# W1 in thirds on two queues, four first units around tile 1's transposes, and a new order of single-tile and paired units up to tile 5

**Chip, cores, metric.** One core of one Trainium2 chip. The time is the device time of that core in microseconds (us). The kernel was already tuned: 207.95 us (median of 3 runs, 207.95 to 208.64) before the change.

## The reference

```python
# x: (1, 2048, 640) bf16; H = 32 heads of 20; F = 1536
xn  = layernorm(x)                                  # no scale, no bias
qkv = xn @ wqkv;  phi(t) = where(t > 0, t + 1, exp(t)) + 1e-6
A   = (phi(q) (phi(k)^T v)) / (phi(q) sum(phi(k)))  @ wo      # linear attention, per head
B   = gelu(xn @ w1 + b1) @ w2 + b2                  # dense block
out = x + A + B
```

## The kernel before

A small planner records instructions for each engine in program order. Each has resources that it reads and writes; the planner makes semaphore waits of them. x comes in 16 tiles of 128 tokens. First, the loads and the start of the dense block: each tile is normalised on VectorE (DVE; the power for rstd, one over the standard deviation, on POOL), transposed on TensorE (PE) and copied to `xnT` (tiles 0 to 3; the others are transposed by DMA), and multiplied with W1. That product is called h below, and k counts the five slices of 128 columns of D that are summed for it. A *unit* is 5 matmuls (k = 0..4) for 128 columns of F and one or more tiles, with its Gelu on ScalarE (ACT).

```python
dma_x(0, 1)
dma_w("scalar", b1tmp[:], ..., r_b1tmp)
dma_w1(0, "scalar")            # W1 in four quarters of 480 KB
dma_x(1, 1); dma_w1(1); dma_x(2, 1); dma_w1(2); dma_x(3, 1); dma_w1(3)
...                            # x tiles 4 to 15

def h_first(jbs):              # tile 0, k 0,1 of all units first, then k 2..4
    bs = [take(1) for _ in jbs]
    for (ks, res) in (((0, 1), r_xnTA), ((2, 3, 4), r_xnT[0])):
        for jb, b in zip(jbs, bs):
            Pl.ins("tensor", [... matmul(bank(b, 0, P), W1[:, k, ...], xnT[:, k, 0:P]) for k in ks],
                   reads=[r_W1[jb * P // FW], res], writes=[B_[b]])
    ...                        # Gelu of each unit

filler(10)                     # warm-up matmuls, N = 512
ln_stats(0); ln_half(1, 0); ln_half(1, 1); ln_aggr(1)
norm0(0, CA, r_xnA); norm0(CA, D, r_xnB)      # tile 0 in two parts
...                            # transposes, copies: first part DVE, second ACT
b1_step(); ln_norm(1)
h_first([0, 1, 2])
```

Second, `units(t0, n, lo, hi)`: units lo..hi of n tiles from t0 on. The last tile's output goes out in three stores (80, 48 and 32 KB), and the program waits for all stores. ACT, which has no work since 133 us, has these waits, but for the last:

```python
stores = [ev for (waits, fns, ev, dma) in Pl.records["sync"][n_sync:] if dma]   # 18
for ev in stores[:-1]:
    Pl.wait_event("scalar", ev)
Pl.wait_event("sync", stores[-1])
```

## Time and profile before

| | before |
|---|---|
| span of the profiled run | 206.8 us, clock 1.0 |
| PE / DVE / ACT busy | 98% / 54% / 35% |
| wait of the chain before PE's first real matmul | W1's first quarter, landed 6.98 us |
| first matmul of the K projection (chain; its own start in the timeline is 60.26) | 60.42 us |
| last DVE instruction | 205.04 to 205.33 us |
| from there to the end of the span | 1.50 us |

The chain names PE for 96% of the span. From 7.03 to 205.02 us it is PE alone, so each us that PE loses there moves the end. The first fence is the view of DMA issues from 200 to 207 us (size, us from issue to landing), the second SyncE's waits of the last four us (us in total, times, longest).

```profile
out_dram<-out_sb SPq DMA_DIRECT2D x1, 48.0 KB, 1.5
out_dram<-out_sb SPq DMA_DIRECT2D x1, 32.0 KB, 1.4
```

```profile
SPq L108 <- DMA out_dram<-out_sb: 1.1, 1, 1.1
```

The last 32 KB take 1.4 us from issue to landing, and the kernel ends when SyncE has seen that.

### The profile page before, as it was taken

How to read it: one execution, taken by the hardware profiler on the slowest of the kernel's cores; microseconds unless marked ns; L12 is line 12 of the kernel's file. 1: busy time of each engine (PE TensorE's matmuls, PEld its weight loads, DVE VectorE, ACT ScalarE, POOL GpSimd, SP SyncE). 2: the span in 40 equal slices, each digit the busy share in tenths (PEclk: the TensorE clock that was granted, in tenths of full speed). 3: DMA queues.
4: the chain of work that ended last, by engine and by line, in shares of the span. 5: the costliest groups of instructions: out<-in, count | busy, mean ns of one | idle time of the engine just before them, and what ended most of it. 6: DMA issues, size and time to landing. Idle time of an engine off the chain costs nothing.

```text
span 206.8 us, 3936 instructions
## 1 busy us (share of the span) xinstructions
PE 203.7 (98%) x1588; PEld 140.6 (68%) x1588; DVE 112.2 (54%) x231; ACT 73.2 (35%) x141; POOL 21.2 (10%) x59
## 2 busy tenths in 40 slices
PE   7999999999999999999999999999999999999996
PEld 2799987444457777777756556677777777777775
DVE  4679970000006888999288888574763522522332
ACT  2589887666676555111153554400000000000000
POOL 3245568000022000000000000000000000000000
PEclk9999999999999999999999999999999999999999
DMA  6999668998000000000300001932112112000002
GB/s 167 344 357 114 105 126 138 375 325 277 3 0 0 0 0 3 0 3 0 63 0 5 0 0 23 370 120 51 63 67 57 55 43 57 32 33 35 32 33 65
DMA packets 23851, 18.32 MB, mean 89 GB/s; under 512 B 10392, under 2 KB 23832, under 8 KB 23832
## 3 DMA queue, kind: packets, MB, share of 16 engines
q1 hardware_dynamic: 23152, 17.57, 30.1%
q10 hardware_dynamic: 680, 0.49, 0.9%
q8 instruction: 12, 0.20, 0.4%
q14 instruction: 7, 0.06, 0.1%
HBM read 12.62 MB, written 2.62 MB: 74 GB/s over the span
## 4 chain that ended last, share of the span: by engine, by line
PE 96%; DMA 3%; ACTq 0%; DVE 0%; issue 0%
PE ps L615 34%; PE ps L352 25%; PE ps L512 11%; PE ps L473 11%; PE ps L524 10%; DMA W<-in_B_w_dram 3%; PE ps L651 2%; PE ps L551 1%; PE ps L533 1%; PE ps L562 1%; PE ps L382 1%; PE ps L336 0%; ACTq L233 0%; DVE out_sb L654 0%
## 5 line engine op out<-in xcount | busy, mean ns | idle before, releaser
L352 PE MATMUL ps<-xnT,W 128*128 128x128 bf16 (+2 forms) x435 | 52.0, 282 | 0.0
L615 PE MATMUL ps<-W,HG 128*128 128x320 bf16 x360 | 51.0, 299 | 0.0
L352 PEld LDWEIGHTS ps<-xnT,W 128*128 128x128 bf16 x435 | 35.6, 98 | 15.6
L615 PEld LDWEIGHTS ps<-W,HG 128*128 128x128 bf16 x360 | 35.1, 98 | 14.2 <-issue 0.4
L356 ACT ACTIVATE HG<-ps,b1c 128x128 bf16<-128x128 f32 (+2 forms) x87 | 40.1, 493 | 12.4 <-PE ps L352 10.3
L634 DVE TENSOR_TENSOR out_sb<-ps,xnT 128x640 bf16<-128x640 f32 x15 | 12.4, 825 | 35.0 <-PE ps L615 34.8
L460 ACT ACTIVATE ek<-ps 128x512 bf16<-128x512 f32 (+1 forms) x36 | 23.2, 645 | 20.3 <-PE ps L524 10.6
L461 DVE TENSOR_SCALAR ek<-ek 128x512 bf16<-128x512 bf16 (+1 forms) x36 | 11.0, 304 | 33.7 <-ACT ek L460 32.5
L615 PE MATMUL ps<-Msb,PQ 128*128 128x320 bf16 x150 | 22.3, 299 | 0.0
L524 PE MATMUL ps<-xnT,Wqkv 128*128 128x512 bf16 x100 | 21.9, 379 | 0.0
L512 PE MATMUL ps<-xPK,xn_tm 128*128 128x320 bf16 x160 | 21.9, 299 | 0.0
L473 PE MATMUL ps<-Wqkv,xnT 128*128 128x320 bf16 x160 | 21.9, 299 | 0.0
L473 PEld LDWEIGHTS ps<-Wqkv,xnT 128*128 128x128 bf16 x160 | 15.7, 98 | 6.2
L512 PEld LDWEIGHTS ps<-xPK,xn_tm 128*128 128x128 bf16 x160 | 15.7, 98 | 6.1
L615 PEld LDWEIGHTS ps<-Msb,PQ 128*128 128x128 bf16 x150 | 14.7, 98 | 5.7
L524 PEld LDWEIGHTS ps<-xnT,Wqkv 128*128 128x128 bf16 x100 | 11.7, 117 | 9.5
L463 DVE SCALAR_TENSOR_TENSOR PQ<-ps,ek 128x512 bf16<-128x512 f32 x20 | 13.8, 692 | 2.1
L308 DVE BATCH_NORM_STATS2 stats<-xPK 128x6 f32<-128x320 bf16 x32 | 13.6, 467 | 1.9 <-DMA xPK<-in_A_x_dram 1.9
L463 DVE SCALAR_TENSOR_TENSOR xPK<-ps,ek 128x640 bf16<-128x640 f32 x16 | 13.2, 824 | 1.7
L499 DVE TENSOR_TENSOR Msb<-Msb,xPK 128x640 f32<-128x640 f32 x14 | 11.6, 826 | 0.5
L318 POOL TENSOR_TENSOR rstd<-aggr,mhalf 128x1 f32<-128x1 f32 x16 | 9.1, 569 | 8.9 <-DVE aggr L316 8.9
L516 ACT ACTIVATE W<-ps 128x640 bf16<-128x640 f32 x5 | 3.5, 704 | 18.2 <-PE ps L512 18.2
(61 smaller groups left out, 94.6 us busy)
## 6 DMA issues: line engine op xcount, KB each, us to landing
xnT<-in_A_x_dram SPq DMA_DIRECT2D x4, 640.0 KB, 6.2
Wqkv<-in_A_wqkv_dram SPq DMA_DIRECT2D x3, 800.0 KB, 6.5
out_dram<-out_sb SPq DMA_DIRECT2D x15, 160.0 KB, 1.8
W<-in_B_w_dram SPq DMA_DIRECT2D x1, 1920.0 KB, 15.2
W<-in_B_w_dram SPq DMA_DIRECT2D x3, 480.0 KB, 6.7
xPK<-in_A_x_dram SPq DMA_DIRECT2D x2, 640.0 KB, 9.0
Wo<-in_A_wo_dram SPq DMA_DIRECT2D x1, 800.0 KB, 10.4
xPK<-in_A_x_dram SPq DMA_DIRECT2D x4, 160.0 KB, 4.1
```

The source lines that it names most:

```text
L308: Pl.ins(v, lambda e: e.bn_stats(stats[:, s, 6 * h:6 * h + 6], x_in[:, t, h * HW:(h + 1) * HW]), reads=[r_x[t]], writes=[r_stats[s][h]])
L352: Pl.ins("tensor", [(lambda e, k=k: e.matmul(bank(b, 0, w), W1[:, k, jb * P:(jb + 1) * P], xnT[:, k, tok], start=(k == 0), stop=(k == DT - ...
L356: Pl.ins("scalar", lambda e: e.activation(HG[:, jb, tok], bank(b, 0, w), ACT.Gelu_apprx_tanh, bias=b1c[:, jb:jb + 1]), reads=[B_[b], r_b1c ...
L460: Pl.ins("scalar", lambda e: e.activation(e2, src, ACT.Exp), reads=br, writes=[r_ek[s]])
L461: Pl.ins(v, lambda e: e.tensor_scalar(et, et, 1.0, 1e-6, ALU.min, ALU.add), reads=[r_ek[s]], writes=[r_ek[s]])
L463: Pl.ins(v, lambda e: e.scalar_tensor_tensor(out=d2, in0=src, scalar=0.0, in1=e2, op0=ALU.max, op1=ALU.add), reads=br + [r_ek[s]], writes= ...
L473: fns.append(lambda e, k=k, h=h, b=b, t=t: e.matmul(bank(b + h, 0, HW), xnT[:, k, t * P:(t + 1) * P], Wqkv[:, k, D + h * HW:D + (h + 1) * ...
L499: Pl.ins(v, lambda e, t=t: e.tensor_tensor(out=zsum, in0=zsum, in1=PK[:, t, :], op=ALU.add), reads=[r_PK[t], r_zsum], writes=[r_zsum])
L512: Pl.ins("tensor", [(lambda e, t=t, h=h, b=b, f=f: e.matmul(bank(b + h, 0, HW), xn_tm[:, t, f * P:(f + 1) * P], PK[:, t, h * HW:(h + 1) * ...
L524: Pl.ins("tensor", [(lambda e, k=k, j=j, b=b: e.matmul(bank(b), Wqkv[:, k, j:D:DT], xnT[:, k, cc], start=(k == 0), stop=(k == DT - 1))) fo ...
L615: return lambda e: e.matmul(bank(b + h, 0, HW), l, r[:, h * HW:(h + 1) * HW], start=(i == 0), stop=(i == JT + DT - 1))
L634: Pl.ins(v, lambda e: e.tensor_tensor(out=halves(out_sb[:, s, :]), in0=pair(b), in1=halves(x_res[:, t, :]), op=ALU.add), reads=B_[b:b + 2] ...
```

## The change

The intent: PE waits for 480 KB of W1 until 6.98. The change splits a first third (640 KB) over the two queues, so that the part with k 0,1 is there early. It gives PE four units of tile 0 with tile 1's transposes in between, brings tile 0's normalisation and the bias's transpose forward, swaps the engines of tile 0's two copies, moves the statistics of the next tile behind the normalisation, in part, from tile 2 on, and reorders the units up to tile 5.

```diff
@@ -202,7 +202,8 @@
         r_xb = [R_("xb%d" % t) for t in range(NT)]
         r_xn = [R_("xn%d" % t) for t in range(NT)]
         r_xnT = [R_("xnT%d" % t) for t in range(NT)]
-        NW1 = 4
+        NW1 = 3
+        r_W1A = R_("W1_0A")
         r_W1 = [R_("W1_%d" % i) for i in range(NW1)]
         r_Wq, r_Wk, r_Wv, r_W2, r_Wo = R_("Wq"), R_("Wk"), R_("Wv"), R_("W2"), R_("Wo")
         r_b1tmp, r_b1c, r_b2 = R_("b1tmp"), R_("b1c"), R_("b2")
@@ -237,15 +238,16 @@
         FW = F // NW1
         def dma_w1(i, eng="sync"):
             dma_w(eng, W1[:, :, i * FW:(i + 1) * FW], w1v[:, :, i * FW:(i + 1) * FW], r_W1[i])
+        KA = 2
         dma_x(0, 1)
         dma_w("scalar", b1tmp[:], B_b1.rearrange("(a p) -> a p", p=P), r_b1tmp)
-        dma_w1(0, "scalar")
+        dma_w("scalar", W1[:, 0:KA, 0:FW], w1v[:, 0:KA, 0:FW], r_W1A)
         dma_x(1, 1)
+        dma_w("sync", W1[:, KA:DT, 0:FW], w1v[:, KA:DT, 0:FW], r_W1[0])
         dma_w1(1)
         dma_x(2, 1)
         dma_w1(2)
         dma_x(3, 1)
-        dma_w1(3)
         dma_x(4, 2)
         dma_x(6, 2)
         for c in range(2, NC):
@@ -375,14 +377,16 @@
                    reads=[res, r_ident], writes=[B_[b]])
             return xnT[:, k0:k1, 0:P], pT[:, 0:(k1 - k0) * P].rearrange("p (k q) -> p k q", k=k1 - k0), b
 
-        def h_first(jbs):
+        def h_first(jbs, between):
             bs = [take(1) for _ in jbs]
             for (ks, res) in (((0, 1), r_xnTA), ((2, 3, 4), r_xnT[0])):
                 for jb, b in zip(jbs, bs):
                     Pl.ins("tensor", [(lambda e, k=k, jb=jb, b=b: e.matmul(
                         bank(b, 0, P), W1[:, k, jb * P:(jb + 1) * P], xnT[:, k, 0:P],
                         start=(k == 0), stop=(k == DT - 1))) for k in ks],
-                        reads=[r_W1[jb * P // FW], res], writes=[B_[b]])
+                        reads=[r_W1A if res is r_xnTA else r_W1[jb * P // FW], res], writes=[B_[b]])
+                    if res is not r_xnTA and jb == jbs[1]:
+                        between()
             for jb, b in zip(jbs, bs):
                 Pl.ins("scalar", lambda e, jb=jb, b=b: e.activation(
                     HG[:, jb, 0:P], bank(b, 0, P), ACT.Gelu_apprx_tanh, bias=b1c[:, jb:jb + 1]),
@@ -391,21 +395,22 @@
         r_xnTA = R_("xnT0A")
         Pl.ins("scalar", lambda e: e.activation(b1c[:, 0:1], warm[:, 0:1], ACT.Gelu_apprx_tanh),
                reads=[r_warm], writes=[r_b1c])
-        filler(10)
+        filler(6)
+        b1_step()
+        filler(3)
         ln_stats(0)
         ln_half(1, 0)
         ln_half(1, 1)
-        ln_aggr(1)
         norm0(0, CA, r_xnA)
         norm0(CA, D, r_xnB)
+        ln_aggr(1)
         dA, sA, bA = transp0(0, 2, r_xnA)
         filler(1)
         dB, sB, bB = transp0(2, DT, r_xnB)
-        Pl.ins(v, lambda e: e.tensor_copy(dA, sA), reads=[B_[bA]], writes=[r_xnTA])
-        Pl.ins("scalar", lambda e: e.activation(dB, sB, ACT.Copy), reads=[B_[bB]], writes=[r_xnT[0]])
-        b1_step()
+        Pl.ins("scalar", lambda e: e.activation(dA, sA, ACT.Copy), reads=[B_[bA]], writes=[r_xnTA])
+        Pl.ins(v, lambda e: e.tensor_copy(dB, sB), reads=[B_[bB]], writes=[r_xnT[0]])
         ln_norm(1)
-        h_first([0, 1, 2])
+        h_first([0, 1, 2, 3], lambda: xnT_copy(1, transp(1)))
 
         TD = 4
         late = Pl.records["sync"][x_done:]
@@ -419,25 +424,25 @@
         def ln_next(t):
             if t + 1 < NT:
                 ln_half(t + 1, 0)
-                ln_half(t + 1, 1)
             ln_norm(t)
             if t + 1 < NT:
+                ln_half(t + 1, 1)
                 ln_aggr(t + 1)
 
-        xnT_copy(1, transp(1))
+        units(1, 1, 0, JQ)
+        units(0, 2, JQ, 2 * JQ + 1)
         ln_stats(2)
-        ln_next(2)
-        units(0, 1, 3, 2 * JQ)
-        units(1, 1, 0, 2 * JQ)
-        units(0, 2, 2 * JQ, 2 * JQ + 2)
+        ln_norm(2)
+        ln_stats(3)
         xnT_copy(2, transp(2))
-        units(0, 2, 2 * JQ + 2, JT)
+        units(0, 2, 2 * JQ + 1, JT)
         ln_next(3)
+        units(2, 1, 0, 3)
+        xnT_copy(3, transp(3))
+        units(2, 1, 3, 6)
         ln_next(4)
-        units(2, 1, 0, JQ)
-        xnT_copy(3, transp(3))
-        units(2, 1, JQ, JT)
-        units(3, 1, 0, JT)
+        units(3, 1, 0, 6)
+        units(2, 2, 6, JT)
         for t in range(TD, NT):
             if t > TD:
                 ln_next(t)
@@ -445,7 +450,10 @@
                    reads=[r_xn[t]], writes=[r_xnT[t]], dma=True)
         Pl.records["sync"] += late
         run_masks(len(mask_jobs))
-        for (t0, n) in [(4, 2), (6, 2), (8, 4), (12, 4)]:
+        units(4, 1, 0, 3)
+        units(5, 1, 0, 3)
+        units(4, 2, 3, JT)
+        for (t0, n) in [(6, 2), (8, 4), (12, 4)]:
             units(t0, n, 0, JT)
```

## The prediction

> **What bounds the kernel now.** I read the page first, then the chain of waits in order of time, then the first 20 us of the timeline, because the diff touches only the first third of the program and its DMA order.
>
> The page gives the busy shares:
> ```profile
> PE 203.7 (98%) x1588; PEld 140.6 (68%) x1588; DVE 112.2 (54%) x231; ACT 73.2 (35%) x141; POOL 21.2 (10%) x59
> ```
> TensorE is the bound and no other engine is near. The chain (start us, length us, what) shows from when it is so:
> ```profile
> 1.46 5.52 DMA W<-in_B_w_dram
> 6.99 0.05 issue
> 7.03 1.07 PE ps L382 x15
> 8.10 0.28 PE ps L336 x5
> 8.38 3.60 PE ps L352 x55
> 11.98 0.28 PE ps L336 x5
> ...
> 15.56 44.86 PE ps L352 x345
> 60.42 21.73 PE ps L473 x160
> ```
> The only wait on it is the first quarter of W1 (480 KB, issued at 1.46, landed at 6.98). From 7.03 to 205.04 it is matmul after matmul without a gap. So the change can pay in two ways only: let the first matmul on real data (L382) start before 7.03, or shorten the matmuls that follow. And it pays only if no new gap opens.
>
> What would hold L382 if W1 were early? The timeline (start, length, engine, what) has the chain of tile 0 beside the load:
> ```profile
> 3.13 0.89 DVE L308 BATCH_NORM_STATS2 stats<-xPK 128x6 f32<-128x320 bf16 x2 [1.93 <-DMA xPK<-in_A_x_dram]
> 4.13 0.21 DVE L316 BATCH_NORM_AGGREGATE aggr<-stats 128x2 f32<-128x12 f32 x1
> 4.25 0.83 DVE L308 BATCH_NORM_STATS2 stats<-xPK 128x6 f32<-128x320 bf16 x2
> 4.42 0.57 POOL L318 TENSOR_TENSOR rstd<-aggr,mhalf 128x1 f32<-128x1 f32 x1 [0.48 <-DVE aggr L316]
> 5.22 0.21 DVE L316 BATCH_NORM_AGGREGATE aggr<-stats 128x2 f32<-128x12 f32 x1
> 5.35 0.71 DVE L365 TENSOR_SCALAR xn_tm<-xPK,aggr,rstd 128x256 bf16<-128x256 bf16 x2
> 5.70 0.39 PE L372 MATMUL ps<-ident,xn_tm 128*128 128x128 bf16 x2
> 6.13 0.29 DVE L404 COPY xnT<-ps 128x256 bf16<-128x256 bf16 x1
> 6.31 0.53 PE L372 MATMUL ps<-ident,xn_tm 128*128 128x128 bf16 x3
> 6.87 0.49 ACT L405 ACTIVATE xnT<-ps 128x384 bf16<-128x384 bf16 x1 [3.48 <-PE ps L372]
> 7.93 0.44 PE L336 MATMUL ps<-ident,xn_tm 128*128 128x128 bf16 x5
> 8.41 0.49 DVE L344 COPY xnT<-ps 128x640 bf16<-128x640 bf16 x1 [1.64 <-PE ps L336]
> ```
> Read down: xnT of tile 0 is complete only at 7.36 (its first two of five slices at 6.42). The W1 wait therefore hides little: the next wait stands right behind it. Note also the last two lines: from transposing tile 1 to its copy in xnT, 7.93 to 8.90, it takes 0.97 us, and TensorE fills this now with single-tile units of tile 0.
>
> [...]
> [...] between first transposes at 8.21 and 11.82 lie 45 matmuls of N=128 and 10 of N=256; between 12.10 and 15.12 lie 15 and 20. Solving the two sums gives 56 ns and 109 ns. [...] The ten warm-up matmuls of N=512 take 0.427 us each here (4.45 us less the last one's tail), so they are cold, and the transposes at 6.31 to 6.63 still start 0.107 us apart; by 7.1 the steps are 0.056. In this run the gate opened between 6.63 and 7.1.
> [...] it moved 329 to 355 GB/s from 4 us on with both queues full[...].
>
> **The change part by part.**
> *W1 in thirds, the first in two pieces.* The stretches of 1 us moved 21, 279, 172, 329, 355, 354, 344, 340, 333 and 341 KB (1-2 us to 10-11 us). Before, W1_1 and the second x tile behind it were complete in this running sum at 6.4 and 6.9 and landed at 7.5 and 8.0: about 1.1 us from moved to landed. After, the first piece is 262 KB (2 of 5 k, 512 columns) on ACT's queue. Before, that queue had moved 491 of some 1120 KB at 5.9, 44%; so 262 KB are done when 595 KB have moved, 4.4 us, and land near 5.5. x0, x1 and both pieces are 983 KB: 5.5, landing 6.6. The second third: 1638 KB, landing 8.5; x2 8.95; last third 10.9; x3 11.4. W1 is off the path, if these estimates hold.
>
> *LayerNorm of tile 0.* The aggregate of tile 1 (5.22) goes behind the two normalisations. These then start when stats and rstd are there, 5.04 instead of 5.35: everything of tile 0 comes 0.31 us earlier. First transposes 5.39, filler, second transposes 6.03 (were 6.31), finished 6.55 still cold. The copies change engines: ACT has the first 256 columns (about 0.39 us, from its 0.49 for 384), 5.82 to 6.2; DVE the other 384 (about 0.36 from its 0.29 for 256 and 0.49 for 640), 6.59 to 6.95. The bias transpose moves in among the warm-up matmuls: b1's 3 KB are long there, and it costs nothing.
>
> *Four first units.* Their 8 matmuls with k 0,1 can start at 6.3, 0.75 us earlier than now. Cold up to about 6.85 and warm afterwards they end at 7.0, which is when the second copy arrives anyway. So most of the 0.75 us is lost to cold clock or to the wait for k 2 to 4. The 6 matmuls of the first two units take 7.0 to 7.34.
>
> *Tile 1's transposes between.* DVE normalises tile 1 behind the copy (now 6.34, then 6.9 to 7.34), so the transposes start at 7.38. Transposed 7.82, copied 7.86 to 8.35. TensorE has only the 6 matmuls of units 3 and 4 to fill this: 7.66 to 8.0. What comes next in program order is tile 1. It waits until 8.41: a new gap of about 0.4 us.
>
> *Units.* Up to the units of tiles 6 and 7: single-tile units 36 become 26 (180 to 130 matmuls of 56 ns), pairs 18 become 23 (90 to 115 of 109 ns). 10.08 + 9.81 = 19.89 becomes 7.28 + 12.54 = 19.82 us: 0.07 less. The 15 transposes stay.
>
> *Sum.* Before: 7.03 + 0.84 (15 transposes) + 19.89 = 27.76 for the start of tiles 6 and 7. After: at 8.41, 20 single matmuls and 5 transposes are done; 110 x 0.056 + 10 x 0.056 + 12.54 = 19.26, giving 27.67. Gain: 0.1 us. Later stages are untouched and PE-bound.
>
> **Later waits.** I walked the rest with the same steps. W1's second third is wanted at 8.4 + 20 x 0.056 = 9.5 and lands at 8.5; the last third is wanted at 11.7 and lands at 10.9. xnT of tile 2 is wanted at 14.2 (there 13.2), of tile 3 at 16.1 (there 16.0: tight). DVE's new order, one half of the next statistics before the normalisation, makes it wait some 0.3 us per tile for rstd from POOL (0.57 us), 1.6 us per tile where it now takes 1.32. Tile 4 is transposed by DMA at about 19.7 and wanted at 21.1; tile 5 at about 21.4 and wanted at 22; tile 15 at 37 and wanted after 40. The loads behind these transposes are for 60 us. No wait, but two margins are thin.
>
> **Rivals.**
> (a) *The W1 wait is worth its whole 0.75 us.* It would be, if the clock opened earlier than 6.3 and the second copy ended by 6.6. [...] Against: the transposes here are cold at 6.5. This would give 207.2 to 207.4.
> (b) *A piece of W1 arrives late* (its second piece is behind two x tiles and shares the engines with ACT's), or DVE's wait for x2 at 8.95 or for rstd delays tile 2, 3 or 5. For it: 172 GB/s at 3 to 4 us shows that the early rate is not steady; the margins above. Each such miss costs 0.2 to 0.5 us: 208.1 to 208.5.
> (c) *Pairs make TensorE much faster.* A page that averages the durations suggests it (219 ns for N=128, 273 ns for N=256)[...]. The starts, 56 and 109 ns, leave 3 ns per pair of matmuls: 0.07 us in all. I reject it.
>
> **The range and the chances.** 207.95 less 0.1 is 207.85. (a) seems to me a little likelier than (b), since the gap in front of tile 1 is the largest single loss and hangs on a clock that may open earlier; I take 207.75. Each rival moves it by up to 0.6 us and the three runs before spread by 0.69: 207.1 to 208.4. For 2% (4.2 us) faster TensorE would have to start at 2.9 us, before the first x tile has landed; 2% slower needs a gap ten times the one foreseen. Both are nearly excluded.
>
> **What would show it.** Right: the wait for W1 is gone, the first h matmul starts near 6.3, a gap of TensorE of about 0.4 us ends near 8.4 with tile 1's copy, and the first k matmul (L473's counterpart, 60.26 now) starts about 0.1 us earlier. Wrong: the chain still has a W1 load in it; no gap before tile 1 (then the gain is 0.5 us); a TensorE gap between 9 and 25 us; or a warm clock long before 6.6.

The sum: it came to 27.76 before and 27.67 after, a gain of 0.1 us, so 207.85, taken as 207.75; the 56 and 109 ns in it are solved from the trace. "Cold", "warm" and "the gate opened" stand for what was measured: transposes that start 0.107 us apart up to 6.63 and steps of 0.056 by 7.1. That the clock may open earlier in another execution was the author's estimate at that time, and so was that new orders of the loads leave the running sum of bytes as it was (from 3.0 to 4.5 us the kernel before moved 219 GB/s, the kernel after 298).

## The result, and the profile after

| | before | after |
|---|---|---|
| time, median of 6 (range) | 208.15 (207.95 to 208.64) | 208.83 (208.44 to 209.16) |
| first matmul of the K projection (chain) | 60.42 | 60.13 |
| last DVE instruction begins | 205.04 | 204.75 |
| from its end to the end of the span | 1.50 | 2.38 |
| span | 206.8 | 207.4 |

The ratio after to before is 1.0028, interval 1.0009 to 1.0047: 0.6 us slower. Here and below, a ratio is the mean time of one kernel's fast runs over that of the other's of the same rounds, so not quite the ratio of the medians.

The chain of the kernel after (start, us, what):

```profile
0.80 2.27 DMA xPK<-in_A_x_dram
...
6.32 0.94 PE ps L384 x14
7.26 0.42 PE ps L338 x5
7.68 0.02 issue
7.70 0.50 DVE xnT L346
8.20 0.05 issue
8.25 4.02 PE ps L354 x45
...
60.13 21.73 PE ps L481 x160
...
204.75 0.29 DVE out_sb L662
```

W1 is gone from it: it begins with the load of x and the normalisation of tile 0. The first h matmul (L384) starts at 6.32 instead of 7.03, then the chain passes through tile 1's copy (L346, 7.70 to 8.20), a piece that the chain before did not have. From 8.25 on it is PE again, and at 60.13 and at the end PE is 0.29 us *ahead* of before. Yet the span is 0.6 us longer. So the loss lies behind the last matmul. The same two views of the end as before, for the kernel after:

```profile
q14 instruction: 2, 0.02, 0.8%
...
out_dram<-out_sb SPq DMA_DIRECT2D x1, 48.0 KB, 1.8
out_dram<-out_sb SPq DMA_DIRECT2D x1, 32.0 KB, 2.3
```

```profile
SPq L108 <- DMA out_dram<-out_sb: 2.0, 1, 2.0
```

The last store takes 2.3 us instead of 1.4, and SyncE waits 2.0 us for it instead of 1.1. The first line is a hint: the profile names queue 14 "instruction", and two packets of it, 8 KB each, came in these last microseconds. Here are the DMA queues of the kernel after in two narrow windows, 205.88 to 206.20 and 206.55 to 206.80 us (packets, MB, share):

```profile
q1 hardware_dynamic: 135, 0.03, 45.5%
q14 instruction: 1, 0.01, 11.4%
```

```profile
q1 hardware_dynamic: 9, 0.00, 3.8%
```

The store has 144 packets: 128 of 256 B and 16 of 4 B, so nine for each of the 16 DMA engines that the profile counts, if they are spread evenly. 135 of them, fifteen such shares, had moved by 206.17. The other nine, eight of 256 B and one of 4 B, came from 206.58 on; no packet began between 206.20 and 206.55. In that time one 8 KB packet of instructions was under way, from 206.00 to 206.59. The trace does not name the engine of a packet; that the late nine are the share of one engine, the one with the fetch, is inferred from these counts. In the kernel before, the nearest such fetches are at 185.85, 198.22 and 202.69, and the 144 packets move in one burst, 206.18 to 206.46 (window 206.10 to 206.50):

```profile
q1 hardware_dynamic: 144, 0.03, 39.0%
```

The second 8 KB in these last microseconds, 204.77 to 205.20 in the kernel after, is there in the traces of after_pad5 and after_pad1 below too, from 205.06 and 205.10 on, so it is not the one that the added ACTIVATEs move. It overlaps the 48 KB store, which takes 1.8 us instead of 1.5; that store is not the last, so the end does not feel it.

Whose instructions? ACT passed a wait (for the 80 KB store) at 204.99, 1.01 us before the fetch began. In the kernel before it was the wait passed at 184.56, and a fetch began at 185.85. ACT has five ACTIVATEs fewer after the change (units of pairs replace single ones: 87 Gelus of units become 81, the first units' 3 become 4), so a fixed place in its stream is reached five instructions later: here five of its instructions that wait for stores. That is the theory to test. In both kernels the packet in question has 8 KB.

### The profile page after: what moved, and what is told of

It is laid out like the page before. It is cut to its first block, busy times and chain, and to the rows that moved or that the text cites. A ratio compares the mean times of both kernels' runs of the same rounds, so it can differ in the third digit from the quotient of the medians.

```text
span 207.4 us, 3885 instructions
## 1 busy us (share of the span) xinstructions
PE 202.9 (98%) x1562; PEld 139.8 (67%) x1562; DVE 113.7 (55%) x231; ACT 72.7 (35%) x136; POOL 21.4 (10%) x59
## 4 chain that ended last, share of the span: by engine, by line
PE 96%; DVE 1%; DMA 1%; issue 0%; DVEq 0%
PE ps L623 33%; PE ps L354 25%; PE ps L520 10%; PE ps L481 10%; PE ps L532 10%; PE ps L659 2%; PE ps L559 1%; DMA xPK<-in_A_x_dram 1%; DVE stats L310 1%; PE ps L541 1%; PE ps L570 1%; PE ps L338 0%; PE ps L384 0%; PE ps L374 0%; DVE xnT L346 0%
## 5 line engine op out<-in xcount | busy, mean ns | idle before, releaser
L354 PE MATMUL ps<-xnT,W 128*128 128x256 bf16 (+2 forms) x405 | 51.6, 290 | 0.3 <-DVE xnT L346 0.3
L354 PEld LDWEIGHTS ps<-xnT,W 128*128 128x128 bf16 x405 | 34.9, 98 | 16.3 <-DVE xnT L346 0.4
L358 ACT ACTIVATE HG<-ps,b1c 128x256 bf16<-128x256 f32 (+2 forms) x81 | 39.2, 508 | 13.2 <-PE ps L354 10.8
L310 DVE BATCH_NORM_STATS2 stats<-xPK 128x6 f32<-128x320 bf16 x32 | 14.7, 469 | 2.8 <-DMA xPK<-in_A_x_dram 2.8
```

What stands on the lines that cost most here:

```text
L310: Pl.ins(v, lambda e: e.bn_stats(stats[:, s, 6 * h:6 * h + 6], x_in[:, t, h * HW:(h + 1) * HW]), reads=[r_x[t]], writes=[r_stats[s][h]])
L354: Pl.ins("tensor", [(lambda e, k=k: e.matmul(bank(b, 0, w), W1[:, k, jb * P:(jb + 1) * P], xnT[:, k, tok], start=(k == 0), stop=(k == DT - ...
L358: Pl.ins("scalar", lambda e: e.activation(HG[:, jb, tok], bank(b, 0, w), ACT.Gelu_apprx_tanh, bias=b1c[:, jb:jb + 1]), reads=[B_[b], r_b1c ...
```

## The experiments

Kernels are compared only within the same rounds. All gave the correct result. "The end" is the time from the end of the last DVE instruction to the end of the span. Six executions, of 210.26 to 210.83 us, have a granted clock of 0.992, all others whose clock is on record at least 0.998: three of the kernel before (one of 210.53), two of before_minus7, one of before_minus8. They count and widen the intervals.

**after_pad5 and after_pad1**: ACT's stream made longer again.

```diff
+        scr = sb("scr", [P, 8], FP32)
...
+        for i in range(5):        # after_pad1: range(1)
+            Pl.ins("scalar", lambda e, i=i: e.activation(scr[:, i:i + 1], warm[:, i:i + 1], ACT.Copy), reads=[r_warm])
         for ev in stores[:-1]:
             Pl.wait_event("scalar", ev)
```

> The kernel after, with five one-column ACTIVATEs added on ScalarE behind its last real work (ScalarE idles there), so that its instruction stream is as long as that of the kernel before. Theory (instruction fetch): in the trace after, TensorE's work ends 0.29 us earlier but the last store lands 2.3 us after its issue instead of 1.4, because 8 KB of instructions were fetched at 206.00 us, right when ScalarE passed its last wait but one, and one of the 16 shares of the store started only at 206.58. With five more instructions that fetch falls about five stores earlier (near 185 us), the last store lands in 1.4 us: 0.6 to 0.9 us faster than the kernel after, 0.2 to 0.4 us faster than the kernel before (207.8 to 208.0 where that has 208.15). Rival (the loss is in the first 60 us and the profiled run is not typical): no change, 208.8. Rival (the tail is chance): the spread stays, mean 208.5 to 208.8.

> The same with one added ACTIVATE. Theory: the fetch moves to the wait before (about 205.0 us), is over by 205.6, and the last store (moving from 205.9) is free of it: as fast as with five, within 0.2 us. If one is not enough but five are, the mark lies elsewhere than I think. Rivals: 208.8.

Measured: after_pad5 208.11 us (207.98 to 208.89), 0.9999 of before (0.9985 to 1.0014); after_pad1 208.07 (207.96 to 208.54), 0.9996 (0.9982 to 1.0009). Against the 1.0028 of the kernel after, about 0.65 us came back by one instruction that does nothing. ACT's fetch began at 185.57 with five and at 204.08 with one, again 1.0 us after a wait was passed; the end took 1.50 us in both. SyncE's last wait in after_pad5:

```profile
SPq L108 <- DMA out_dram<-out_sb: 1.1, 1, 1.1
```

The expectation also had 0.2 to 0.4 us *less* than before; that did not come. What the change wins at the start is too small to be seen: K began at 60.43 and 60.47 in these traces, against 60.42 before. One reason is in after_pad1's timeline (start, us, engine, what, wait):

```profile
7.22 0.51 PE L385 MATMUL ps<-xnT,W 128*128 128x128 bf16 x6 [0.23 <-DMA W<-in_B_w_dram]
```

W1's second piece, issued at 1.73, landed at 7.17 here and took 5.4 us; in the kernel after's own trace it took 4.2. W1 then holds PE as before the change.

**after_rerun and after_pool**: the kernel after unchanged, and with the waits moved away from ACT, on one chip.

```diff
-            Pl.wait_event("scalar", ev)
+            Pl.wait_event("gpsimd", ev)      # after_pool
```

> The kernel after, unchanged, on one chip with the three others. All seven other traces so far take 1.50 us from the last VectorE instruction to the end, its own took 2.38. Theory (ScalarE's instruction fetch meets the last store): this trace again shows an 8 KB fetch about 1.0 us after ScalarE passed its wait for the store before the last but one, and 2.1 to 2.4 us at the end; 0.5 to 0.8 us slower than the kernel before. Rival (one chance event in the first trace): 1.5 us and the time of the kernel before, 208.1.

> The kernel after with all 17 waits for stores moved from ScalarE to POOL; no instruction of work is added. Theory: ScalarE's stream ends with the copies near 133 us, no fetch of it falls into the last store; 1.5 us at the end, 0.5 to 0.8 us faster than after_rerun. Rival (the added ACTIVATEs, not the place of the fetch, made the end short): as slow as after_rerun.

Measured: after_rerun 208.84 us (208.57 to 210.15), 1.0023 (0.9982 to 1.0064); its end took 2.16 us, with 135 packets up to 206.28, a fetch from 206.13 to 206.60, and the other nine from 206.60 on. after_pool 208.13 (207.84 to 208.33), 0.9975 (0.9935 to 1.0015), end 1.51 us. The kernel before had two runs of 210.6 and 210.8 us, both at a clock of 0.992, hence the wide intervals: without them its mean is 208.35, and the plain means of the two kernels are 209.08 and 208.12. Beside each other their medians differ by 0.7 us, and every run of after_rerun is longer than every run of after_pool. It is neither chance nor the added ACTIVATEs.

**before_minus5, 7, 8, 9**: the same from the other side, no work changed in the kernel before.

```diff
-        for ev in stores[:-1]:
-            Pl.wait_event("scalar", ev)
+        for i, ev in enumerate(stores[:-1]):
+            Pl.wait_event("gpsimd" if i < 5 else "scalar", ev)      # or 7, 8, 9
```

> The kernel before with the first five of ScalarE's waits for stores moved to POOL, which idles: no work is changed, ScalarE's stream is five instructions shorter, as in the kernel after. Theory: the fetch that came at 185.85 us now comes near the last store, which lands in 2.0 to 2.4 us instead of 1.4: 0.5 to 0.9 us slower than before (208.7 to 209.0). Rivals: same time as before, 208.15.

> As before_minus5, but seven waits moved to POOL. In before_minus5 ScalarE passed the wait at 199.06 us and 8 KB were fetched 1.0 us later, clear of all stores: five was too few, so it tested nothing. Two more place the mark on the wait for the store before the last but one, as in the kernel after (there passed at 204.99, fetch at 206.00, last store's packets from 205.90). Theory: fetch and last store meet, from the last VectorE instruction to the end it takes 2.1 to 2.4 us instead of 1.50, and the time is 0.4 to 0.9 us over the kernel before (208.5 to 209.0). If they just miss each other (the fetch comes some 0.03 us later against the store than in the kernel after), the end takes 1.5 us. Rival (the length of the end does not hang on the fetch): 1.5 us although the fetch lies within the last store.

> As before_minus7 with one wait more moved: there ScalarE passed the mark at 203.19 us and the fetch ran from 204.20 to 204.77, still one wait too early. Theory: it now comes with the wait at 205.3 to 205.6, the fetch at 206.3 to 206.6, where the last store's packets move from 206.2: 2.1 to 2.4 us at the end, 0.4 to 0.9 us slower than before. If the fetch starts after the last packets (it would be 0.1 us later than in the kernel after), 1.5 us and no difference. Rival: 1.5 us although the fetch lies within the packets.

> The kernel before with nine of ScalarE's waits for stores moved to POOL: two waits share one instruction, so this is five instructions fewer, as in the kernel after. Theory: ScalarE passes the mark with its wait for the store before the last but one (205.3 us), the fetch runs from about 206.3, the last store's packets from 206.2; if they meet, 2.1 to 2.4 us at the end instead of 1.50 and 0.4 to 0.9 us slower than before. If the fetch comes after the one share that would wait for it, 1.5 us and no difference: then the collision is a matter of less than 0.2 us. Rival (the end depends on something else in the kernel after): 1.5 us although one share of the store waits for the fetch.

The first three missed their aim. before_minus5: 208.32 us, 1.0004 (0.9988 to 1.0019), fetch at 200.07, end 1.50. before_minus7: 209.01 (207.97 to 210.81), 1.0040 (0.9990 to 1.0090), fetch at 204.20, end 1.50; two of its unprofiled runs, 210.26 and 210.81, have the clock of 0.992, and why the other four go from 207.97 to 209.18 is open. before_minus8: 208.28 (208.07 to 210.33), 1.0000 (0.9954 to 1.0045), fetch at 206.36 in a profiled run that was late as a whole (last store's packets from 208.40), end 1.51. The trace shows two waits in one instruction of ACT (in ten of its last eleven in the kernel before), so that seven and eight moved waits alike shifted the fetch by four stores, and five by three.

With nine, a shift by five, it was hit: 208.99 us (208.82 to 209.13), 1.0026 (1.0011 to 1.0040), end 2.20 us. Its DMA queues from 206.20 to 206.60 and from 206.93 to 207.10 us (no packet began between 206.60 and 206.93), and the last store:

```profile
q1 hardware_dynamic: 135, 0.03, 36.8%
q14 instruction: 1, 0.01, 7.3%
```

```profile
q1 hardware_dynamic: 9, 0.00, 5.6%
```

```profile
out_dram<-out_sb SPq DMA_DIRECT2D x1, 32.0 KB, 2.1
```

It is the picture of the kernel after, 135 packets and nine late ones behind a fetch, and the same loss, in a kernel whose start and units are those of before. With this the cause of the slowdown is shown in both directions.

**before_w1**: the split of W1 alone.

```diff
-        NW1 = 4
+        NW1 = 3                      # first third in two pieces on two queues, as in the change
...
-        JQ = JT // NW1
+        JQ = 3                       # order of units as before
```

> The kernel before with W1 alone changed: thirds, the first in two pieces on two queues; order of units, LayerNorm and ScalarE's instruction count stay. Theory from my prediction: the first h matmul starts at about 6.45 instead of 7.03, then waits for the second copy at 7.36, so TensorE's later work (first K matmul at 60.26 before) is 0.1 to 0.3 us earlier, and so is the end: 207.85 to 208.05. Rival (the W1 wait is worth all it shows): 0.6 us faster, 207.55. Rival (thirds arrive too late for a later unit): slower, with a new TensorE gap before 13 us.

Measured: 209.46 us (208.62 to 210.01), 1.0056 (1.0036 to 1.0077), K at 61.91. The third way that I had named holds, and more strongly than I thought. The first h matmul started at 7.01, not at 6.45: in the order of before PE had the last transposes of tile 0 from 6.43 and the bias's from 6.89, so the earlier W1 won nothing. From its timeline:

```profile
9.23 3.50 PE L354 MATMUL ps<-xnT,W 128*128 128x128 bf16 x50 [0.39 <-DMA W<-in_B_w_dram]
12.00 0.89 DVE L310 BATCH_NORM_STATS2 stats<-xPK 128x6 f32<-128x320 bf16 x2 [1.14 <-DMA xPK<-in_A_x_dram]
13.29 0.45 PE L338 MATMUL ps<-ident,xn_tm 128*128 128x128 bf16 x5 [0.56 <-DVE xn_tm L331]
```

With thirds, unit 4 needs the second third, which lands only at 9.2. And x3 lands just before 12.0, behind more of W1; since DVE takes tile 3's statistics before it normalises tile 2, PE has no tile 2 to transpose until 13.29. The other parts of the change look made to repair this; the two tests that follow show it for the order of the statistics in a trace, and for none in time. The order of the units was not tested alone.

**after_oldln, after_old0**: after_pad5 with one of those parts put back.

```diff
 # after_oldln: tiles 2 to 15                    # after_old0: tile 0
-        ln_stats(2); ln_norm(2); ln_stats(3)    -        norm0(...); norm0(...); ln_aggr(1)
+        ln_stats(2); ln_next(2)                 +        ln_aggr(1); norm0(...); norm0(...)
 # ln_next: both halves, then ln_norm            # copies: first on DVE, second on ACT
```

> The kernel after with the five added ACTIVATEs, and with VectorE's order for tiles 2 to 15 put back to that of before: tile 3's statistics ahead of tile 2's normalisation. In before_w1 that order made tile 2 wait for tile 3's load (landed near 12 us), a TensorE gap of 0.83 us. Theory: the same gap here, since x3 lands at 11.3 or later: 0.4 to 0.9 us slower than after_pad5 (208.5 to 209.0), so this part is needed only because W1 in thirds delays the x tiles. Rival (the order matters for POOL's rstd alone): 0 to 0.2 us faster than after_pad5, since VectorE no longer waits for rstd.

> The kernel after with the five added ACTIVATEs, and with tile 0's chain put back: tile 1's aggregate ahead of tile 0's normalisation, first copy on VectorE, second on ScalarE. Theory: the chain of tile 0 and then tile 1 comes 0.2 to 0.35 us later, no load hides it any more, and the end follows: 208.3 to 208.5. Rival (W1's second piece is the bound at the start, as in the trace of after_pad1, where it landed at 7.17): same as after_pad5.

after_oldln: 208.38 us (208.13 to 208.98), 1.0009 (0.9969 to 1.0048). The gap is there, but smaller than expected, because x3 landed at 11.1. From its timeline:

```profile
11.12 0.89 DVE L311 BATCH_NORM_STATS2 stats<-xPK 128x6 f32<-128x320 bf16 x2 [1.15 <-DMA xPK<-in_A_x_dram]
12.40 0.28 PEld L339 LDWEIGHTS ps<-ident,xn_tm 128*128 128x128 bf16 x5 [0.33 <-DVE xn_tm L332]
```

PE waits 0.33 us for tile 2. In this trace tile 1's units began at 8.33, 0.22 us before those of after_pad5, whose clock opened later (the last warm-up matmul took 0.38 us here, 0.63 there), and K still began at 60.44 against 60.43: the order costs some 0.2 us there. In time it is not told from after_pad5. after_old0: 208.19 (208.11 to 208.44), 0.9993 (0.9958 to 1.0028): no loss seen. Its trace has tile 0's normalisation at 5.41 instead of 5.13, but its last warm-up matmul already took 0.38 us, that of after_pad5 0.63, so a warm clock may have made up for it: tile 1's copy starts at 8.00 in the one and 8.01 in the other. What this part is worth at an equal clock stays open.

**after_split (run twice) and after_split_pool**: the new gap made smaller.

```diff
-        h_first([0, 1, 2, 3], lambda: xnT_copy(1, transp(1)))
+        h_first([0, 1, 2, 3], copy1)       # two tensor_copy: k 0,1 -> r_xnT1A, k 2..4 -> r_xnT[1]
...
-        units(1, 1, 0, JQ)
+        ...                                # 4 units of tile 1, all k 0,1 first, then k 2..4
```

> The kernel after with the five added ACTIVATEs, and tile 1's copy split in two (k 0,1 then k 2 to 4), its first four units ordered as tile 0's: all matmuls with k 0,1, then those with k 2 to 4. Theory: the TensorE gap of 0.47 us between starts, which ends with tile 1's copy, shrinks by 0.2 us (the copy of 256 columns takes 0.29 instead of 0.49); first K matmul 0.2 us earlier than in after_pad5 at the same clock phase; 0.2 us faster than after_pad5 and the kernel before (207.9). Rival (the gap is not on the path): no change.

> after_split again, since its chip gave one outlier and a wide interval (0.9982, 0.9944 to 1.0019). Theory: 0.2 us faster than the kernel before (0.9985 to 0.9995), 0.8 us faster than after_rerun; first matmul of tile 1 some 0.2 us earlier than in after_rerun's trace at the same clock phase.

> The kernel after with tile 1's copy split and the waits for stores on POOL, no added instructions of work. Theory: both gains, 0.2 us from the split and the undisturbed end, so 207.7 to 207.9 like after_split, 0.2 to 0.4 us faster than before. Rival (POOL's own fetch or its waits disturb the end): 208.1 or more.

after_split, which has the five ACTIVATEs too: 207.91 us (207.65 to 208.90), 0.9982 (0.9944 to 1.0019). Again: 207.80 (207.61 to 207.92), 0.9960 (0.9924 to 0.9996), where the two runs of before at a clock of 0.992 (210.6 and 210.8) count; without them the plain means are 207.78 and 208.35, and in the first call, without its one, 208.01 and 208.14. In the first trace:

```profile
8.04 0.56 DVE L420 COPY xnT<-ps 128x256 bf16<-128x256 bf16 x2 [0.60 <-PE ps L339]
8.38 1.01 PE L445 MATMUL ps<-xnT,W 128*128 128x128 bf16 x15
```

PE starts tile 1 at 8.38, 0.34 us after the copy began; in after_pad5, whose clock was as cold (the last warm-up matmul took 0.63 us in both), at 8.55, 0.54 us after. K begins at 60.26 and 60.14, 0.16 to 0.28 us before that of the kernel before (and no earlier than in the kernel after's own traces, 60.13 and 60.25, where the clock opened earlier: 0.38 us for that matmul). In the medians after_split is 0.22 and 0.65 us faster than the kernel before, and 0.33 us faster than after_pool. after_split_pool, without added instructions, was to confirm it and did not: 0.9997 (0.9976 to 1.0019), five fast runs from 207.64 to 209.00, its profiled run slow (238.10), so its start isn't told from a trace. Its rival had named POOL's waits: in the two kernels with all 17 waits there, the time is 1.24 to 1.60 us longer than the span, in all others 1.20 to 1.33. But its fast spans are no shorter than those of before (207.1 in both medians), so that alone does not explain it. So that the split makes the kernel faster is likely from the trace, but not shown in time by all three.

## Why the prediction was wrong

It said 207.75 us, 207.1 to 208.4; the kernel took 208.83.

- **The step that failed** is the last sentence of the sum: "Later stages are untouched and PE-bound." They are PE-bound (the chain is PE from 8.25 to 204.72), but the program has a piece after PE, 1.50 us of it, that I never looked at, and neither did any of the three rivals. It became 2.38 and 2.16 us. The count of units, by which I reckoned 0.07 us on PE, also took five instructions from ACT, which I reckoned at nothing because ACT idles. They moved an instruction fetch of ACT from 185.85 us to 206.00, onto the last store, of which one sixteenth, nine of 144 packets, came late. Shown by after_pad1 and after_pad5 (gone with one added instruction), after_pool (gone with none), after_rerun (there again) and before_minus9 (there without the change).
- **The start** was right in its steps. W1 off the path, first h matmul near 6.3: it was 6.32. A gap that ends near 8.4 with tile 1's copy: it ended at 8.25, the copy on the chain, and in after_pad5, with a later clock (the last warm-up matmul 0.63 us, not 0.38), at 8.55. Gain of 0.1 us: 0.29 and 0.17 us at the first K matmul in the two traces of the kernel after, about 0 in after_pad5, after_pad1 and after_pool (60.38 to 60.47). So the larger gain of the first trace is luck, at least in part: its clock opened early (0.38 us, below) and W1 was there. With the end repaired the three took 208.07 to 208.13 us, inside the range; beside the kernel before that is 0.9999, 0.9996 and 0.9975 (0.9989 by the plain means without its two runs at 0.992).
- **Units:** the change of some 0.07 us is too small to be tested by times. The sum over all units holds: it has 19.26 us for the kernel after from tile 1's units to those of tiles 6 and 7, and 60.42 - 27.76 = 32.66 us more to K, 51.92 in all; measured from 8.25 to 60.13 it is 51.88.
- **Rival (a)**, an earlier clock: in the kernel after's own trace the last warm-up matmul takes 0.38 us, where it took 0.63 before:

```profile
5.59 0.38 PE L297 MATMUL ps<-warm 128*128 128x512 bf16 x1
```

  So the clock was open by then, one of the signs that I had named of being wrong. At the first K matmul it brought 0.29 us, not the 0.55 to 0.75 of the rival: the first h matmul came 0.71 us earlier, and then the chain shows the wait for tile 1's copy.
- **Rival (b)**, a late piece of W1, happened in after_pad1 (7.17 instead of about 6.6 as estimated) and, for the kernel with W1 alone changed, cost 1.5 us at K together with the late x3. The landing times that I worked out from one trace are good to about 0.7 us. The later waits did not come about: the chain of the kernel after has none between 8.25 and the end.

## What to carry to other kernels

When PE is the bound, look also at what comes after its last instruction (1.50 us here), and at what else moves there (8 KB of instructions here). The change of instruction counts on an engine without work moved an instruction fetch, from 185.85 to 206.00 us, and with one ACTIVATE added the last store was free of it (1.4 us to landing again); if a result turns by half a microsecond for no reason of its own, find the instruction packets in the trace, and keep an engine with nothing to do from running through waits at the very end. And when a wait is taken off the front of the chain, ask first what ended just behind it: here 0.7 us of wait were worth 0 to 0.3.

## What else the traces show

- A fetch for an engine that has no work left delayed another queue's store: while one packet of 8 KB took 0.47 to 0.59 us, nine of the store's 144 packets stood back, and the store landed in 2.1 to 2.3 us instead of 1.4 (kernel after, after_rerun, before_minus9).
- On queue 14, where the packets taken for ACT's came, instructions came in 8 KB within the span, on queue 8 in 16 KB (kernels before and after). ACT's began 1.0 to 1.3 us after it passed the wait at which the place was reached (1.01 in the kernel after, 1.29 in the kernel before).
- In before_minus8 the clock was open early: the last warm-up matmul took 0.38 us, and the granted clock was 1.00 from 4.30 to 7.70. Then it was 0.50 for 3.40 us, after a stretch in which PE was busy for 1.66 of 3.40 us and its longest wait, for W1, was 1.10 us (stretch, PE busy, ..., granted clock, DMA share, GB/s):

```profile
4.30:7.70 3.40, 1.66 (x12) 0.61 (x11) 2.20 (x8) 0.56 (x2) 1.35 (x3) 1.00 0.99 308
7.70:11.10 3.40, 3.40 (x33) 3.40 (x34) 1.07 (x3) 1.38 (x5) 0.09 (x1) 0.50 1.09 358
```

  So the granted clock fell though no single wait of PE in that stretch was over 1.10 us; what set it off is not shown. From 11.10 to 14.00 it was 1.00 again. That run took 210.33 us, with K at 62.64. The kernel before had three runs of 210.5 to 210.8 us without a trace; they and two of before_minus7 (210.26 and 210.81) have the same granted clock as this run, 0.992, where all others on record have at least 0.998. An estimate from this trace agrees: 3.40 us at 0.50 lose 1.70 us of clock, 0.8% of the span of 209.1. All six have the start of the kernel before, and none of the runs with the new start has it; whether the new start prevents it is not shown.
- Early loads scatter: the same 384 KB, issued at 1.73 us, took 4.2, 4.3 and 5.4 us (kernel after, after_pad5, after_pad1).
